# A channel-attention and highway kernel: score banks, load groups, chain order and the last store rearranged

## The chip, the cores and the metric

The kernel runs on one core of a Trainium2 chip. The metric is the device time of one execution in microseconds; a kernel's time is the median of several runs. The core has five engines, each with an instruction queue of its own that is worked in order: TensorE (PE in the profile; PEld is its weight load), VectorE (DVE), ScalarE (ACT), GpSimd (POOL) and SyncE (SP). DMA engines move data between memory and the core's SBUF; SyncE, ScalarE and GpSimd issue them. TensorE writes into PSUM, of which the kernel uses all eight banks.

## The reference

For each of B = 4 batches of N = 6336 rows and C = 256 columns, the columns of q and k are normalised over the rows, and a 256 by 256 attention over the columns is made and applied to v; a highway layer follows on all 25344 rows:

```
qn = q / (norm(q, axis=1) + 1e-6);  kn = k / (norm(k, axis=1) + 1e-6)
s  = kn^T @ qn / tau;  a = softmax(s)          # (B, 256, 256)
x  = v @ a                                     # (B, N, 256) -> (B*N, 256)
H  = relu(x @ w_h);  T = sigmoid(x @ w_t + b_t)
out = T * H + (1 - T) * x
```

## The kernel before

**Scores.** The 6336 rows of a batch are 49 tiles of 128 rows and one of 64. For each tile j, `emit_score` (L192) adds k^T q to the bank S (two 128 by 256 matmuls), k^T k to the bank G (two 128 by 128), and q^T q to G (two more), whose diagonals are the squared norms. Instead of the two q^T q matmuls, runs of four tiles may be squared on ScalarE (`square`, L395), added on GpSimd and reduced on VectorE; `decide` (L368) chooses as the program is written out. Batches 1 to 3 use the same two banks S and G as batch 0, one after the other.

**Chain.** After a batch's last score, `make_chain` (L436) builds its attention: the norms out of G (VectorE, L448), a copy of S (`ssb`, ScalarE, L463), roots, inverses, a small matmul that spreads the inverse norms of q (`cq`, L502), the scaled logits (L507), exp on ScalarE (L518, with a table load before it and `back`, L603, which loads the sigmoid's table after it), the normalised attention (`softmax`, L524, into `mr`), its transpose (`at`, L539, copied by `at_copy`, L550), and the product of attention and the highway's weights (`ah`, L558, copied by `ahat_copy` into `mr`). With that, a tile of v needs three products alone: v a, v a w_h and v a w_t.

**Slots.** A slot t is a pair of v tiles. Its work: four transposes (T, L234) into one PSUM bank, a copy to SBUF (C, L248), twelve 256-column matmuls into Z, H and X (the gate's, the hidden and the plain product, `mains`, L253), the sigmoid on ScalarE (tt, L301), a refill of the Z bank with the bias (seed, L304), two operations on VectorE (th, L309 and ux, L317), a subtraction on GpSimd (L335; the last one on VectorE) and a store for each four pairs (L351, from SyncE's queue; the last four pairs each have their own). There are 25 slots a batch; in batch 3 the slot with the 64-row tile comes 21st. Z has two banks of its own; H and X take the oldest free bank of a list, hx0 to hx2 (`free_bank`, L278), which `cq`, `at` and `ah` share. After the last chain, S and G join this list (L1014).

**Order.** The instruction order is written out by a planner at build time (L995 on): it steps through time with lengths that the program gives each task, and each engine takes the first task of its lists that is ready. TensorE (`step_pe`, L903) prefers chain tasks, then scores that are due, then transposes, then the slot's matmuls. A score of batch b + 1 is due at a slot that `slot_of_score` (L631) spreads evenly up to `S_END`, so that a batch's scores run between the slots of the batch before it. On the chip, each engine follows its list in order and waits where the data are late.

**Loads.** q, k and v are loaded by GpSimd in groups of tiles (`QG`, `VG`, L95), with a conversion from f32 to f16; q and k have four buffers each, v three. A load waits until the scores (or transposes) have read the group four (three) before. The list `order` (L624) fixes the order of the loads: after batch 0's groups the first group of batch 1, then the two weights, the first group of v, the next group of batch 1, and so on. A store can be put behind a GpSimd instruction, so as to leave the DMA engines to the loads.

Of the kernel before, what the change touches and what calls it, by code (L numbers as in the profile page):

```python
# [60 lines left out]
def kernel(  # L61
# [33 lines left out]
    QG = [spans(4, 8, 8, 8, 8, 8, 3, 2)] + [spans(4, 12, 12, 12, 9)] * (B - 1)  # L95
# [11 lines left out]
    S_END = [19, 44, 69]  # L107
# [84 lines left out]
    def emit_score(b, j):  # L192
        if j == 0:
            S_t[b] = psum_pool.tile([P, 2, C], f32, tag="S", name=f"S{b}")
            G_t[b] = psum_pool.tile([P, 4, P], f32, tag="G", name=f"G{b}")
# [78 lines left out]
    banks = [Bank(f"hx{n}") for n in range(3)]  # L274
    late_banks = [Bank("S"), Bank("G")]
    in_late = [False]

    def free_bank(now):  # L278
        pool = banks + (late_banks if in_late[0] else [])
        got = [x for x in pool if x.free(now)]  # L280
        if not got:
            return None
        return min(got, key=lambda x: max([t.end for t in x.until], default=-1.0))
# [57 lines left out]
    def emit_store(b, i0, n, behind):  # L341
# [6 lines left out]
        else:  # L348
            parts = [(rows(ob)[:, 2 * i0 : 2 * (i0 + n), :], ot[:, o0 : o0 + 2 * n, :])]
        for dst, src in parts:  # L350
            dma = nc.sync.dma_start(out=dst, in_=src)  # L351
# [84 lines left out]
    def make_chain(b):  # L436
# [166 lines left out]
        add("back", "ACT", 1.5, lambda e: preload_table(Act.Sigmoid), [(T["exps", 1], 0.0)])  # L603
        for c in range(2):
            add(("softmax", c), "DVE", 0.5, softmax(c), [(T["exps", c], LAG)])
            add(("at", c), "PE", 2 * MM(P), pe_at(c), [(T["softmax", c], TO_PE)],
                bank=lambda c=c: [T["atc", c]])
            add(("atc", c), "DVE" if c == 0 else "ACT", 0.4, at_copy(c), [(T["at", c], PE_LAG)])
            add(("ah", c), "PE", 2 * MM(2 * C), pe_ahat(c), [(T["atc", c], TO_PE)],
                bank=lambda c=c: [T["ahc", c]])  # L610
            add(("ahc", c), "ACT" if c == 0 else "DVE", 0.62, ahat_copy(c),
                [(T["ah", c], PE_LAG)])
        return T
# [14 lines left out]
    order += [(-80, "q", 1, 0), (-80, "k", 1, 0), (-79, "w", 0, 0), (-79, "w", 0, 1)]  # L628
    order += [(-70, "v", 0, 0), (-69, "remv", 0, 0), (2, "remq", 0, 1), (2, "remk", 0, 1)]

    def slot_of_score(b, j):  # L631
        lo = (b - 1) * NPAIR - 1 if b > 1 else -3
        return lo + (S_END[b - 1] - lo) * j / NS

    for b in range(1, B):
        for g in range(len(QG[b])):
            if (b, g) == (1, 0):
                continue
# [126 lines left out]
    for b in range(B):  # L765
        for j in range(NS + 1):
            t = score[b, j]
            if j == 0 and b > 0:
                t.after += [(chains[b - 1]["norms"], TO_PE), (chains[b - 1]["ssb"], TO_PE)]

    for t in range(NSLOT):
# [27 lines left out]
        queues["PE.out"] += [Z[t], H[t], X[t]]  # L799
# [103 lines left out]
    def step_pe(now):  # L903
# [10 lines left out]
        if look < 2 and take("PE.T", "PE", now):  # L914
# [10 lines left out]
    def step_act(now):  # L925
# [4 lines left out]
        if ptr["copy"] - slot_now() < ahead and take("copy", "ACT", now, 0.58):  # L930
# [136 lines left out]
```

## Time and profile before

| | us |
|---|---|
| median of 3 runs (277.8 to 278.63) | 278.09 |
| the profiled execution | 278.24 |
| its span, first to last instruction | 276.5 |
| TensorE busy, 2656 matmuls | 252.2 (91%) |
| weight loads busy | 219.0 (79%) |
| VectorE busy | 203.7 (74%) |
| GpSimd busy | 198.0 (72%) |
| ScalarE busy | 173.1 (63%) |
| 23 stores of 1024 KB, median from issue to landing | 9.7 |
| mean granted clock of TensorE (1 is full) | 0.990 |

The profiled execution took 278.24 us, 1.7 more than its span. All times in the text are counted from the span's start, in this one execution. Busy is the time in which at least one instruction of the engine is drawn; the ends of matmuls are modelled, and neighbours overlap. A row of the timeline gives the start, the length, the engine, the line and operation, what is written and read, and in brackets the idle time before it and what ended it. A row by stage gives the stretch, its length, the busy time of PE, PEld, DVE, ACT and POOL with their instructions, the granted clock, the DMA engines' share and what they moved in GB/s. In the slices, each digit is the busy share of one of 40 equal slices in tenths.

### The profile page before, as it was taken

To read this page: it belongs to the slowest core of one execution; us is meant where nothing else is said; L and a number is where in the kernel's file an instruction comes from. 1 tells how busy PE (TensorE), PEld (TensorE's weight loads), DVE (VectorE), ACT (ScalarE), POOL (GpSimd) and SP (SyncE) were. 2 spreads that over 40 slices of the span, in tenths; PEclk is the share of its full clock that TensorE was granted. 3 is DMA by queue.
4 is the path that set the end of the run, shared out by engine and by line. 5 is a ranking of instruction groups with operands and counts; after the bars stand their busy time and mean duration, and the time that the engine had idled before them with its cause. 6 is when DMAs were issued, how large, how long until landed. Compare 5 with 4: busy or idle time off the path is not lost.

```text
span 276.5 us, 6636 instructions
## 1 busy us (share of the span) xinstructions
PE 252.2 (91%) x2656; PEld 219.0 (79%) x2656; DVE 203.7 (74%) x422; ACT 173.1 (63%) x286; POOL 198.0 (72%) x208
## 2 busy tenths in 40 slices
PE   0997887999999999999999999999999979999980
PEld 0696774889899886999999985999999857999770
DVE  2000046598969789979888887989988899998891
ACT  3300036676666487957656587667775787999850
POOL 5133552789979656998998575998898368888870
PEclk9999999999999999999999999999999999999996
DMA  7999999999999999999999999999999997594353
GB/s 213 216 211 216 202 212 213 214 213 215 214 217 215 247 268 275 269 296 297 265 244 219 287 247 256 281 294 288 284 213 259 373 313 243 88 310 191 152 218 117
DMA packets 15281, 66.10 MB, mean 239 GB/s; under 512 B 1681, under 2 KB 4242, under 8 KB 12306
## 3 DMA queue, kind: packets, MB, share of 16 engines
q0 software_dynamic: 10176, 38.67, 70.5%
q1 hardware_dynamic: 4930, 26.48, 24.1%
q10 hardware_dynamic: 144, 0.52, 0.5%
q8 instruction: 21, 0.34, 0.4%
q14 instruction: 10, 0.08, 0.1%
HBM read 78.38 MB, written 25.95 MB: 377 GB/s over the span
## 4 chain that ended last, share of the span: by engine, by line
PE 68%; DMA 20%; DVE 6%; ACT 1%; issue 1%; POOL 1%; DVEq 0%
PE x L258 13%; PE zbank L258 13%; PE h L258 13%; DMA k<-in_k_dram 13%; PE S L203 12%; PE vtps L234 6%; PE G L206 6%; DMA v<-in_v_dram 6%; PE G L212 3%; DMA qk<-in_k_dram 2%; DVE th L309 1%; DVE vts L248 1%; DVE mr L532 1%; DVE ux L317 1%; DVE ssb L507 1%
## 5 line engine op out<-in xcount | busy, mean ns | idle before, releaser
L335 POOL TENSOR_TENSOR o<-th,ux 128x512 f32<-128x512 f32 x95 | 121.7, 1296 | 33.1 <-DVE ux L317 31.2
L258 PEld LDWEIGHTS <-vts 128*128 128x128 f16 x1200 | 111.7, 98 | 17.9 <-issue 5.8
L301 ACT ACTIVATE tt<-zbank 128x512 f32<-128x512 f32 x100 | 59.4, 597 | 52.8 <-PE zbank L258 30.8
L203 PE MATMUL S<-q,k 128*128 128x256 f16 x392 | 82.1, 279 | 11.0 <-ACT k L753 6.4
L309 DVE SCALAR_TENSOR_TENSOR th<-h,tt 128x512 f32<-128x512 f32 (+1 forms) x104 | 68.8, 665 | 18.2 <-ACT tt L301 14.1
L206 PE MATMUL G<-k 128*128 128x128 f16 x392 | 74.1, 223 | 0.6 <-DVE junk L448 0.6
L317 DVE SCALAR_TENSOR_TENSOR ux<-tt,x 128x512 f32<-128x512 f32 (+1 forms) x104 | 67.9, 656 | 1.8 <-PE x L258 1.8
L258 PE MATMUL zbank<-mr,vts 128*128 128x256 f16 (+1 forms) x400 | 60.7, 273 | 0.7 <-DVE mr L573 0.7
L258 PE MATMUL x<-mr,vts 128*128 128x256 f16 (+1 forms) x400 | 60.5, 273 | 0.4 <-DVE ssb L507 0.4
L258 PE MATMUL h<-mr,vts 128*128 128x256 f16 (+1 forms) x400 | 60.5, 273 | 0.0
L304 ACT COPY zbank<-btb 128x512 f32<-128x512 f32 x98 | 57.8, 590 | 2.9
L203 PEld LDWEIGHTS <-k 128*128 128x128 f16 x392 | 39.1, 100 | 16.7 <-ACT k L753 6.4
L206 PEld LDWEIGHTS <-k 128*128 128x128 f16 x392 | 39.2, 100 | 1.8 <-issue 0.8
L234 PE MATMUL vtps<-ident,v 128*128 128x128 f16 x392 | 38.2, 219 | 1.7 <-DVE vts L248 1.4
L248 DVE COPY vts<-vtps 128x512 f16<-128x512 f16 x85 | 35.5, 418 | 5.2 <-PE vtps L234 4.3
L403 POOL TENSOR_TENSOR sq<-sq 128x512 f32<-128x512 f32 (+1 forms) x25 | 30.1, 1208 | 4.3 <-ACT sq L397 4.2
L234 PEld LDWEIGHTS <-v 128*128 128x128 f16 x392 | 27.7, 98 | 5.3 <-issue 3.4
L448 DVE SCALAR_TENSOR_TENSOR junk<-G,ident 128x128 f32<-128x128 f32 x16 | 4.7, 291 | 32.8 <-PE G L212 32.3
L212 PE MATMUL G<-q 128*128 128x128 f16 x192 | 27.4, 226 | 0.0
L154 POOL DMA_DIRECT2D q<-in_q_dram x22 | 12.2, 552 | 20.0 <-PE G L212 18.9
L397 ACT ACTIVATE sq<-q 128x1024 f32<-128x1024 f16 x25 | 26.2, 1054 | 0.0
L410 DVE TENSOR_REDUCE sq<-sq 128x256 f32<-128x768 f32 x25 | 25.7, 1029 | 0.5 <-POOL sq L403 0.3
(67 smaller groups left out, 138.7 us busy)
## 6 DMA issues: line engine op xcount, KB each, us to landing
out_dram<-o SPq DMA_DIRECT2D x23, 1024.0 KB, 9.7
v<-in_v_dram POOLq DMA_DIRECT2D x10, 768.0 KB, 15.8
q<-in_q_dram POOLq DMA_DIRECT2D x9, 768.0 KB, 21.4
k<-in_k_dram POOLq DMA_DIRECT2D x9, 768.0 KB, 22.5
v<-in_v_dram POOLq DMA_DIRECT2D x4, 832.0 KB, 20.6
q<-in_q_dram POOLq DMA_DIRECT2D x5, 512.0 KB, 11.1
k<-in_k_dram POOLq DMA_DIRECT2D x5, 512.0 KB, 13.1
q<-in_q_dram POOLq DMA_DIRECT2D x3, 576.0 KB, 23.7
```

Of the source, the lines that this page charges most:

```text
L203: nc.tensor.matmul(S[:, c, :], kc, qq[0:nr, :], start=first and c == 0, stop=last and c == 1)
L206: nc.tensor.matmul(G[:, c, :], kc, kc, start=first and c == 0, stop=False, skip_group_check=True,)
L212: nc.tensor.matmul(G[:, 2 + c, :], qc, qc, start=False, stop=last and c == 1, skip_group_check=True)
L234: nc.tensor.transpose(ps[:, u, c, 0:r], vt[0:r, bass.ts(c, P)], ident[0:r, 0:r])
L248: cp(out=sb, in_=ps)
L258: nc.tensor.matmul(dst[0:r, u, :], vT_t[t][:, u, kt, 0:r], mr[:, kt, off : off + C], start=(not seeded and kt == 0 and (u == 0 or i == NPA ...
L301: nc.scalar.activation(out=tts[t], in_=zbank[t % 2], func=Act.Sigmoid)
L304: nc.scalar.copy(out=zbank[t % 2], in_=btb)
L309: nc.vector.scalar_tensor_tensor(out=ths[t][pr, us, :], in0=hx["h", t][pr, us, :], scalar=0.0, in1=tts[t][pr, us, :], op0=AluOp.max, op1=A ...
L317: nc.vector.scalar_tensor_tensor(out=uxs[t][pr, us, :], in0=tts[t][pr, us, :], scalar=1.0, in1=hx["x", t][pr, us, :], op0=AluOp.subtract, ...
L335: ins = sub.tensor_tensor(out=ot[pr, o0 + us.start : o0 + us.stop, :], in0=ths[t][pr, us, :], in1=uxs[t][pr, us, :], op=AluOp.subtract,)
L403: nc.gpsimd.tensor_tensor(out=sq[:, 1 : 1 + half, :], in0=sq[:, 1 : 1 + half, :], in1=sq[:, 1 + CH - half : 1 + CH, :], op=AluOp.add,)
```

## The change

- Batch 1's scores get the banks hx1 and hx2 instead of S and G, and batches 2 and 3 use those too. The list of banks for H, X and the chain's products begins with hx0 alone; S and G join it when batch 0's chain has read them, hx1 and hx2 when the last chain has.
- Batch 1's scores no longer wait for batch 0's norms and copy of S. Batch 1's groups of q and k are 4, 4, 12, 12, 12 and 5 tiles instead of 4, 12, 12, 12 and 9, and the second group is loaded ahead of the weights and the first v.
- Scores are due one slot earlier (`S_END` 18, 43, 68 for 19, 44, 69), and the spread of a batch's scores begins after the end of the batch before it.
- In the chain, both softmax steps stand ahead of the copies of `at`, and both `at` ahead of both `ah`; in batch 0, the sigmoid's table is loaded after the copies of `ah`.
- During slot 0, ScalarE and VectorE hold back v copies and square runs where a chain task is soon due.
- The last store is issued from ScalarE's queue. The last slot's Z matmuls stand ahead of the X matmuls of the slot before, and in the last six slots transposes may run three slots ahead.

```diff
--- before.py
+++ after.py
@@ -92,7 +92,8 @@
         assert s0 == NS
         return got
 
-    QG = [spans(4, 8, 8, 8, 8, 8, 3, 2)] + [spans(4, 12, 12, 12, 9)] * (B - 1)
+    QG = [spans(4, 8, 8, 8, 8, 8, 3, 2), spans(4, 4, 12, 12, 12, 5)]
+    QG += [spans(4, 12, 12, 12, 9)] * (B - 2)
     VG = [spans(8, 8, 8, 12, 13)] + [spans(12, 12, 12, 13)] * (B - 1)
     GT = {"q": 12, "k": 12, "v": 13}
     CH = 4
@@ -104,7 +105,7 @@
     OG = 4
     LASTS = list(range(20)) + [NPAIR - 1] + list(range(20, NPAIR - 1))
     PAIRS = [list(range(NPAIR))] * (B - 1) + [LASTS]
-    S_END = [19, 44, 69]
+    S_END = [18, 43, 68]
 
     ctx.enter_context(tc.manual_schedule())
     const_pool = ctx.enter_context(tc.tile_pool(name="consts", bufs=1))
@@ -191,8 +192,9 @@
 
     def emit_score(b, j):
         if j == 0:
-            S_t[b] = psum_pool.tile([P, 2, C], f32, tag="S", name=f"S{b}")
-            G_t[b] = psum_pool.tile([P, 4, P], f32, tag="G", name=f"G{b}")
+            tags = ("S", "G") if b == 0 else ("hx1", "hx2")
+            S_t[b] = psum_pool.tile([P, 2, C], f32, tag=tags[0], name=f"S{b}")
+            G_t[b] = psum_pool.tile([P, 4, P], f32, tag=tags[1], name=f"G{b}")
         nr = REM if j == NS else P
         kk, qq = tile_of("k", b, j), tile_of("q", b, j)
         S, G = S_t[b], G_t[b]
@@ -271,13 +273,11 @@
         def free(self, now):
             return all(t.end is not None and t.end + LAG <= now for t in self.until)
 
-    banks = [Bank(f"hx{n}") for n in range(3)]
-    late_banks = [Bank("S"), Bank("G")]
-    in_late = [False]
+    banks = [Bank("hx0")]
+    handed = []
 
     def free_bank(now):
-        pool = banks + (late_banks if in_late[0] else [])
-        got = [x for x in pool if x.free(now)]
+        got = [x for x in banks if x.free(now)]
         if not got:
             return None
         return min(got, key=lambda x: max([t.end for t in x.until], default=-1.0))
@@ -347,8 +347,9 @@
             ]
         else:
             parts = [(rows(ob)[:, 2 * i0 : 2 * (i0 + n), :], ot[:, o0 : o0 + 2 * n, :])]
+        queue = nc.scalar if (b, i0 + n) == (B - 1, NPAIR - 1) else nc.sync
         for dst, src in parts:
-            dma = nc.sync.dma_start(out=dst, in_=src)
+            dma = queue.dma_start(out=dst, in_=src)
             if behind is not None:
                 tc.add_manual_dep(
                     dma.ins, behind.ins.name,
@@ -600,16 +601,24 @@
             add(("logits", c), "DVE", 0.38, logits(c), [(T["cq"], PE_LAG), (T["ssb"], LAG)])
             add(("exps", c), "ACT", 0.72 + (1.3 if c == 0 and b > 0 else 0), exps(c),
                 [(T["logits", c], LAG), (T["invs", "k"], LAG)])
-        add("back", "ACT", 1.5, lambda e: preload_table(Act.Sigmoid), [(T["exps", 1], 0.0)])
+        back = lambda: add("back", "ACT", 1.5, lambda e: preload_table(Act.Sigmoid),
+                           [(T["exps", 1], 0.0)])
+        if b > 0:
+            back()
         for c in range(2):
             add(("softmax", c), "DVE", 0.5, softmax(c), [(T["exps", c], LAG)])
+        for c in range(2):
             add(("at", c), "PE", 2 * MM(P), pe_at(c), [(T["softmax", c], TO_PE)],
                 bank=lambda c=c: [T["atc", c]])
+        for c in range(2):
             add(("atc", c), "DVE" if c == 0 else "ACT", 0.4, at_copy(c), [(T["at", c], PE_LAG)])
             add(("ah", c), "PE", 2 * MM(2 * C), pe_ahat(c), [(T["atc", c], TO_PE)],
                 bank=lambda c=c: [T["ahc", c]])
+        for c in range(2):
             add(("ahc", c), "ACT" if c == 0 else "DVE", 0.62, ahat_copy(c),
                 [(T["ah", c], PE_LAG)])
+        if b == 0:
+            back()
         return T
 
 
@@ -625,16 +634,17 @@
     for g in range(len(QG[0])):
         order += [(-100 + g, "q", 0, g), (-100 + g, "k", 0, g)]
     order += [(-94.5, "remq", 0, 0), (-94.5, "remk", 0, 0)]
-    order += [(-80, "q", 1, 0), (-80, "k", 1, 0), (-79, "w", 0, 0), (-79, "w", 0, 1)]
+    order += [(-80, "q", 1, 0), (-80, "k", 1, 0), (-79, "q", 1, 1), (-79, "k", 1, 1)]
+    order += [(-78, "w", 0, 0), (-78, "w", 0, 1)]
     order += [(-70, "v", 0, 0), (-69, "remv", 0, 0), (2, "remq", 0, 1), (2, "remk", 0, 1)]
 
     def slot_of_score(b, j):
-        lo = (b - 1) * NPAIR - 1 if b > 1 else -3
+        lo = S_END[b - 2] + 1 if b > 1 else -3
         return lo + (S_END[b - 1] - lo) * j / NS
 
     for b in range(1, B):
         for g in range(len(QG[b])):
-            if (b, g) == (1, 0):
+            if b == 1 and g < 2:
                 continue
             at = slot_of_score(b, QG[b][g][0]) - 1.0
             order += [(at, "q", b, g), (at, "k", b, g)]
@@ -765,7 +775,7 @@
     for b in range(B):
         for j in range(NS + 1):
             t = score[b, j]
-            if j == 0 and b > 0:
+            if j == 0 and b > 1:
                 t.after += [(chains[b - 1]["norms"], TO_PE), (chains[b - 1]["ssb"], TO_PE)]
 
     for t in range(NSLOT):
@@ -796,7 +806,9 @@
             if n >= ORING:
                 for s in store_of_group[o_groups[n - ORING]]:
                     SUB[t].after.append((s.dma, LAG))
-        queues["PE.out"] += [Z[t], H[t], X[t]]
+        queues["PE.out"] += [Z[t], H[t], X[t]] if t < NSLOT - 1 else [H[t], X[t]]
+        if t == NSLOT - 1:
+            queues["PE.out"].insert(len(queues["PE.out"]) - 3, Z[t])
         queues["PE.T"].append(TR[t])
         queues["copy"].append(CP[t])
         queues["ACT.tt"].append(TT[t])
@@ -911,7 +923,7 @@
             if b == 0 or slot_of_score(b, j) <= t:
                 if take("PE.S", "PE", now):
                     return True
-        if look < 2 and take("PE.T", "PE", now):
+        if look < (2 if t < NSLOT - 6 else 3) and take("PE.T", "PE", now):
             return True
         if take("PE.out", "PE", now):
             return True
@@ -927,13 +939,16 @@
             if take(n, "ACT", now):
                 return True
         ahead = 3 if slot_now() >= ACT_COPIES and ptr["copy"] % 2 == 0 else 1
-        if ptr["copy"] - slot_now() < ahead and take("copy", "ACT", now, 0.58):
+        wait = slot_now() == 0 and soon("ACT", now, 0.58)
+        if not wait and ptr["copy"] - slot_now() < ahead and take("copy", "ACT", now, 0.58):
             return True
-        return not soon("ACT", now, 1.05) and take("ACT.sq", "ACT", now)
+        return slot_now() > 0 and not soon("ACT", now, 1.05) and take("ACT.sq", "ACT", now)
 
     def step_dve(now):
         if take("DVE.chain", "DVE", now):
             return True
+        if slot_now() == 0 and soon("DVE", now, 0.42):
+            return False
         ahead = 1 if slot_now() >= ACT_COPIES and ptr["copy"] % 2 == 0 else 3
         if ptr["copy"] - slot_now() < ahead and take("copy", "DVE", now, 0.42):
             return True
@@ -941,7 +956,7 @@
             return True
         if take("copy", "DVE", now, 0.42):
             return True
-        return not soon("DVE", now, 1.0) and take("DVE.red", "DVE", now)
+        return slot_now() > 0 and not soon("DVE", now, 1.0) and take("DVE.red", "DVE", now)
 
     landing = []
     nload = [0]
@@ -1011,11 +1026,12 @@
             seed_banks()
             preload_table(Act.Sqrt)
             setup_done[0] = True
-        if not in_late[0] and chains[B - 1]["norms"].end is not None and \
-                chains[B - 1]["ssb"].end is not None:
-            in_late[0] = True
-            late_banks[0].until = [chains[B - 1]["ssb"]]
-            late_banks[1].until = [chains[B - 1]["norms"]]
+        for b, key, tag in ((0, "ssb", "S"), (0, "norms", "G"), (B - 1, "ssb", "hx1"),
+                            (B - 1, "norms", "hx2")):
+            if tag not in handed and chains[b][key].end is not None:
+                handed.append(tag)
+                banks.append(Bank(tag))
+                banks[-1].until = [chains[b][key]]
         for e, f in (("PE", step_pe), ("ACT", step_act), ("DVE", step_dve),
                      ("POOL", step_pool), ("SP", step_sp)):
             while free[e] <= now and f(now):
```

## The prediction

> **What bounds the kernel now.** I read the page's shares and slices first, then busy time by stage, then TensorE's timeline where a stage lost time, then the chain that ended last and the landing times of the loads.
>
> ```profile
> PE 252.2 (91%) x2656; PEld 219.0 (79%) x2656; DVE 203.7 (74%) x422; ACT 173.1 (63%) x286; POOL 198.0 (72%) x208
> ...
> PE   0997887999999999999999999999999979999980
> ...
> DMA  7999999999999999999999999999999997594353
> ```
>
> Two resources are full at once: TensorE from about 37 us to the end, the DMA engines up to slice 33 (228 us). By stage (sum of PE busy is the first figure after the length; the last two are DMA share and GB/s):
>
> ```profile
> 37.40:51.50 14.10, 10.61 (x101) 7.72 (x99) 8.58 (x30) 10.23 (x19) 5.30 (x8) 1.00 1.10 212
> ...
> 95.80:111.00 15.20, 14.59 (x145) 11.38 (x143) 13.90 (x37) 11.60 (x21) 8.81 (x10) 1.00 1.04 271
> ...
> 156.00:173.00 17.00, 16.31 (x163) 12.82 (x161) 14.55 (x39) 13.52 (x25) 10.04 (x12) 1.00 1.04 257
> 173.00:215.00 42.00, 42.00 (x467) 38.57 (x465) 38.34 (x65) 28.87 (x44) 36.73 (x33) 1.00 1.02 267
> 215.00:231.00 16.00, 14.33 (x127) 10.42 (x125) 15.06 (x45) 12.57 (x23) 9.61 (x9) 1.00 0.94 318
> ```
>
> After 37.4 us TensorE idles only where a batch's softmax chain runs: 3.49 us in batch 0's, 0.61, 0.69 and 1.67 in the others. A 256-column matmul is drawn 0.27 long but issued every 0.11, so each wait costs about 0.16 more than its drawn idle: 8, 3, 3 and 5 waits make 4.8, 1.1, 1.1 and 2.5 us lost. The first chain, in TensorE's timeline:
>
> ```profile
> 37.27 0.27 PE L212 MATMUL G<-rem_q 64*128 64x128 f16 x2
> 38.05 0.27 PE L203 MATMUL S<-q,k 128*128 128x256 f16 x1 [0.51 <-ACT ssb L463]
> 38.94 0.22 PE L206 MATMUL G<-k 128*128 128x128 f16 x1 [0.62 <-DVE junk L448]
> ...
> 40.15 0.65 PE L502 MATMUL cq<-dcat,taus 128*128 128x256 f32 x2
> ...
> 41.22 0.40 PE L234 MATMUL vtps<-ident,v 128*128 128x128 f16 x4
> 42.13 0.38 PE L234 MATMUL vtps<-ident,v 128*128 128x128 f16 x4 [0.52 <-DVE vts L248]
> ...
> 46.47 0.49 PE L258 MATMUL zbank<-mr,vts 128*128 128x256 f16 x3 [0.67 <-DVE mr L573]
> ```
>
> Batch 1's first scores wait for batch 0's to leave the two banks: (0.51 + 0.16) + (0.62 + 0.16) = 1.45 us. But loads pace TensorE here too, as the chain in order of time (start, length) shows, and late q/k loads have little to spare; the load of batch 3's last k group, issued at 179.1, is the 26.1 below and lands at 205.2, and its first score starts at 206.1:
>
> ```profile
> 36.17 15.58 DMA v<-in_v_dram
> 52.04 22.01 DMA k<-in_k_dram
> ```
>
> ```profile
> L154 POOL DMA_DIRECT2D k<-in_k_dram x1: 550/550/550, 179.1 to 179.1; - x1
> ...
> DMA to landing us min/median/max: 23.6/24.8/26.1
> ```
>
> [...]what stands behind a waiting one waits too, and the trace agrees (G at 38.94 holds all scores after it). [...]no trace before shows a store on ScalarE's queue.[...] the trace's four-matmul groups start 0.44 apart[...].
>
> **Early stage, 37.4 to 76.5.** Removed: the 1.45 us. Added: a 4-tile q and k group (q1_1, k1_1) ahead of the weights and v. In the trace 38 tiles' worth of bytes (64 KB each) landed between 37.12 and 49.07, 0.314 us a tile. So k1_1 lands at 37.12 + 8 x 0.314 = 39.6, the weights at 40.9, the first v at 43.4 (41.2 before), k1_2 at 51.6. The changed program's order is scores 0-5, cq, scores 6-7, at0, T0, at1, ah0, ah1, T1, gates. Scores 0-3 take 37.4 to 39.1 (0.43 each); 4-5 wait 0.6 for k1_1 and end at 40.4; cq is behind them, so 0.25 later than the 40.15 before. From cq to the first at of before is 42.72 - 40.15 = 2.57 us: at0 at 43.0, after cq and two scores (1.1 us), an idle of 1.4. T0 waits 0.3 for v, ah0 and ah1 0.3, the first gate 0.7 for the copy of ah1, the third slot 0.5 for a bank that th and ux free. Sum 3.8 to 4.0 where 4.8 was: -0.9. The loads cap it: scores 32 on need k1_4, by which 8 more tiles have landed than at the k load of 74.05 before, 74.05 + 8 x 0.31 = 76.5. The old program does the same work (one more slot 1.31, one transpose 0.22, four more unsquared scores 1.75) by 74.1 + 3.3 = 77.4. Gain 0.8. Bounds: loss 0.5, if k1_1's queue has a bubble of 1.3 us; gain 2.0, if T0 and the third slot wait for nothing.
>
> **Chains.** Both softmaxes now precede the at copy on VectorE, and both at precede both ah on TensorE. In batch 1's order, cq is followed on TensorE by 5.05 us of other work until at0, while softmax 0 ends about 4.7 after cq (logits from 0.64, 1.28 table load, two exps), and at1 has 1.5 us more between. I find no wait left but the slow issue at the 64-row tile, which stays. I take 1.0 of 1.1 for batch 1 and 0.8 of 1.1 for batch 2, where one score group comes close to its load. Bounds: nothing, and 2.2. ACT's sq.2.4 (1.05) now stands ahead of batch 1's exps, covered by those 5.05. For batch 3, T74 waits for a copy behind softmax 1, 1.15 us, and T75 for another, 0.57: 1.7 where 2.5 was, -0.8; bounds 0 and -2.0.
>
> **Squares.** The order shows one more run (26 of them for 25): 8 G matmuls of 0.055 go from TensorE, -0.44. It adds 1.05 to ACT, 1.2 to POOL and 1.03 to VectorE, which are 63, 72 and 74% busy; without that cover at most +1.0.
>
> **Tail.** The last four stores land in 3.6 to 4.2 us each, 0.6 apart as they are issued, so they queue behind nothing; the last is issued at 270.64, right after the last subtract. From ScalarE's queue, empty by then, the same: 0 (0.6 at most if rings do queue; -0.2 to lose). The last Z ahead of the previous X lets tt start 0.44 sooner, but VectorE is back to back from 266.75 with th, ux, th, ux and the subtract; th waits 0.06 for tt now. -0.1. X98 slips 0.44, to end when ux98 can take it.
>
> **Loads in the second half.** Scores end one slot earlier, so they need q and k sooner. The order of k3_4 and v2_3 (13 tiles) is exchanged, so k3_4 lands 13 x 0.31 = 4.0 earlier, 201.2. From there the old program needs 276.5 - 206.1 = 70.4; the new one has five gate groups (2.19) and a transpose (0.22) more to do after it, and 0.9 less of waits: the span cannot end before 201.2 + 71.9 = 273.1. The terms so far, -0.8 - 1.8 - 0.8 - 0.44 - 0.1 = -3.94, give 272.6. With this and k3_1 and k3_3, moved alike, I add 0.8 (bounds 0 and 4).
>
> Sum: -3.14 on a profiled run of 278.24 (span 276.5, 1.7 around it) gives 275.1; the median of the runs is 278.09, 0.15 lower, so 275.0.
>
> **Rivals.** (a) The chains and the early stage give all that they lose, loads keep up: 2.0 + 2.2 + 1.2 + 0.4 = 5.8, about 272.3. For: covers are long. Against: DMA share above 1.0 until 210. 0.20. (b) k1_1 arrives a microsecond late and cq with it, so the chain of batch 0 slips whole: the early gain turns into a loss of 0.5, 276.3. For: it is issued at 35.1 behind a ring slot and the queue is short then. 0.15. (c) Loads take back everything: TensorE only moves its idle time to batches 2 and 3, 278, within 0.3%. 0.10. (d) Slower: stores, which start as TensorE runs ahead, take the place that k3_4 gained. Break-even is a first score of k3_4 at 276.5 - 71.9 = 204.6; from 205.4 on it is slower by over 0.3% (0.83 us, about what a measurement can tell). At 206.5 it gives 280. Against: stores keep their places behind the subtracts. 0.10.
>
> **How the numbers follow.** The forecast has 0.45. Faster: 0.45 + 0.20 + 0.15 = 0.80; same 0.10; slower 0.10. The range leaves out (d) and the best of (a): 272.5 to 278.3.
>
> **What would show it.** Scores without a gap at 37.4, then a short wait for k at 39.1; T0 after 43.4; batch 1's and 2's chains with under 0.3 us idle; PE matmuls 2648; k3_4 landing near 201 with its score right behind it; the last store 3.6 us from issue to landing. Wrong if k1_1 lands after 41, or if TensorE waits over 1 us for k in batches 2 and 3.

## The result and the profile after

The changed kernel takes 278.32 us (median of 4 runs, 278.19 to 278.45) where the kernel before takes 278.01 beside it (4 runs, 277.8 to 278.63). The ratio is 1.0007, 95% interval 0.999 to 1.0025: no difference, where 275.0 was forecast. The profiled execution after took 278.45 us with a span of 276.7; before, 278.24 and 276.5. Runs of one kernel fall into groups some 1 to 2 us apart, so a median also depends on how many runs fell into each, and I give spans where it matters.

From the page of the kernel after, the shares and the slices that answer to those of before:

```profile
PE 252.1 (91%) x2648; PEld 218.8 (79%) x2648; DVE 205.9 (74%) x422; ACT 174.4 (63%) x288; POOL 200.5 (72%) x211
...
PE   0997886999999989999999999999999979999980
...
DMA  7999999999999999999999999999999989783352
```

The eight matmuls are gone and every other total is within 3 us of what it was. By stage (columns as in the prediction: stretch, its length, PE, PEld, DVE, ACT, POOL busy, granted clock, DMA share, GB/s; the first row is a stretch that the prediction did not show):

```profile
30.00:40.00 10.00, 8.33 (x108) 7.54 (x108) 2.19 (x14) 1.84 (x4) 5.95 (x11) 1.00 1.07 179
37.40:51.50 14.10, 10.72 (x95) 7.77 (x93) 7.37 (x27) 8.22 (x17) 6.31 (x12) 0.88 1.12 207
95.80:111.00 15.20, 13.81 (x148) 11.71 (x146) 14.32 (x36) 10.08 (x18) 9.68 (x11) 1.00 1.04 275
156.00:173.00 17.00, 16.56 (x178) 13.86 (x176) 16.20 (x41) 12.79 (x22) 11.05 (x12) 1.00 1.03 270
173.00:215.00 42.00, 41.98 (x454) 37.79 (x453) 37.79 (x69) 29.38 (x46) 35.89 (x32) 1.00 1.02 270
215.00:231.00 16.00, 14.46 (x129) 10.97 (x128) 14.72 (x41) 13.13 (x24) 9.80 (x10) 1.00 0.94 294
```

Batch 0's chain idles 3.38 us (3.49 before), batch 1's 1.39 (0.61 before), batch 2's 0.44 (0.69), batch 3's 1.54 (1.67). A gain in two chains has paid for a loss in another, and the idle time of the early stage has stayed where it was. Two readings matter: the 179 GB/s of the first row, and in the second row the clock of 0.88, where before had 1.00. The first row in the kernel before:

```profile
30.00:40.00 10.00, 7.79 (x100) 7.05 (x101) 2.17 (x14) 1.85 (x4) 7.15 (x12) 1.00 1.19 206
```

To count in one currency, I take each matmul at its undisturbed issue time (the median from start to start: 109 ns for 256 columns and 56 for 128 in both traces, 216 for 512 in that of after) and call TensorE's time beyond that a loss. The two f32 matmuls of a cq I counted at 0.43 us each, twice what the traces show (they issue them 0.22 apart), so every row with a chain stands 0.4 us too low, before and after alike. A stretch without a wait can come out below nothing (-0.31 in a row of before), so I take each figure as good to about 0.3 us. Losses in us:

| stretch | before | after | predicted change | change |
|---|---|---|---|---|
| 37.4 to 80, early stage | 5.78 | 6.25 | -0.8 | +0.5 |
| 80 to 120, chain of batch 1 | 1.39 | 2.10 | -1.0 | +0.7 |
| 120 to 173, chain of batch 2 | 1.54 | 0.63 | -0.8 | -0.9 |
| 173 to 215 | -0.31 | 0.35 | +0.8 for loads | +0.7 |
| 215 to 240, chain of batch 3 | 3.29 | 2.83 | -0.8 | -0.5 |
| matmuls saved | | | -0.44 | -0.45 |

The sum is +0.05, and the span's end, below, adds 0.16: 0.2, which is the difference of the two spans. These are two executions; in others with the same loads (runs 1, 5, 9 and 12) the early stage loses 5.8 to 6.5 us, so there it is nothing to 0.7 us worse than before, and nowhere better.

**Where the early stage went.** TensorE's timeline of the kernel after:

```profile
40.43 0.28 PE L205 MATMUL S<-q,k 128*128 128x256 f16 x1 [0.99 <-DMA k<-in_k_dram]
...
41.10 0.65 PE L503 MATMUL cq<-dcat,taus 128*128 128x256 f32 x2
...
43.55 0.28 PE L544 MATMUL at<-ident,mr 128*128 128x128 f16 x2 [1.14 <-DVE mr L533]
...
44.93 0.40 PE L236 MATMUL vtps<-ident,v 128*128 128x128 f16 x4 [1.10 <-DMA v<-in_v_dram]
```

The scores run without a gap from 37.4 on, as meant. Then they wait 0.99 for k1_1, which lands at 40.4 and not at 39.6; cq follows at 41.10 (40.15 before), and T0 waits 1.10 for a v that lands at 44.9 (43.4 forecast, 41.2 before). The loads are late because of their queue. GpSimd's issues in the kernel after, and then in the kernel before:

```profile
35.11 0.53 POOL L155 DMA_DIRECT2D q<-in_q_dram  x1 [3.24 <-PE G L214]
...
36.15 0.75 POOL L751 DMA_DIRECT2D wht<-in_moe_w_h_dram  x1
...
37.58 0.58 POOL L155 DMA_DIRECT2D v<-in_v_dram  x1
```

```profile
31.84 0.73 POOL L741 DMA_DIRECT2D wht<-in_moe_w_h_dram  x1
...
33.28 0.56 POOL L154 DMA_DIRECT2D v<-in_v_dram  x1
```

The load of q1_1 (batch 1's second group of q) waits 3.24 us for batch 0's matmuls to free a q buffer, and the weights and v, which need no q buffer, stand behind it. They go out 4.3 us later than before. In that gap the DMA engines run short, at 179 GB/s for 206: over 10 us that is 270 KB, 4.1 tiles of 64 KB, or 1.3 us at the prediction's 0.314 us a tile, an estimate.

**Where batch 1's chain went.** The chain in order of time (start, length) of the kernel after:

```profile
98.51 1.81 DVE dcat L494 x2
100.47 0.67 PE cq L503 x2
...
158.12 1.34 DVE dcat L494 x2
159.50 0.70 PE cq L503 x2
```

The two scalings that make `dcat` (an identity times the inverse norms, 128 by 128 each) take 1.81 and 1.34 us together. The same instructions before and after, by tile (minimum, median and maximum in ns):

```profile
L493 DVE TENSOR_SCALAR dcat<-ident,inv x8: 279/284/288, 39.2 to 218.2; 128x128 f32<-128x128 f32 x8
```

```profile
L494 DVE TENSOR_SCALAR dcat<-ident,inv x8: 274/286/1130, 39.2 to 217.0; 128x128 f32<-128x128 f32 x8
```

Nothing about them is changed but the moment. GpSimd's timeline after, at that moment:

```profile
98.28 1.28 POOL L335 TENSOR_TENSOR o<-th,ux 128x512 f32<-128x512 f32 x1
99.52 0.72 POOL L404 TENSOR_TENSOR sq<-sq 128x256 f32<-128x256 f32 x1
```

The first dcat starts at 98.51, 0.23 after a subtract; the subtract ends at 99.56, and 0.08 later, at 99.64, so does dcat (1.13 us). The second ends at 100.32, behind the addition that ended at 100.24. At 158.12 the same happens with one subtract. Before, none of the eight dcat had GpSimd arithmetic beside it. So it is VectorE that waits: each of these three dcat ends 0.08 to 0.09 us behind the GpSimd operation that was under way, while the subtracts beside them take 1.28 us, as they do elsewhere (1.29 on the average of 95). What in the hardware makes it wait the trace doesn't show. So cq waited 1.19 and 0.60 us, by start to start, with all of TensorE's later work behind it. `mr`, the same kind of instruction, meets a subtract in both kernels: at 104.72 it takes 1.38 us after, where 0.35 is its time alone, and at 104.54 0.91 us before.

### The profile page after: what moved, and what is told of

Read it like the earlier page. It is cut to its first block, busy times and chain, and to the rows that moved or that the text cites. A ratio compares the mean times of both kernels' runs of the same rounds, so it can differ in the third digit from the quotient of the medians.

```text
span 276.7 us, 6628 instructions
## 1 busy us (share of the span) xinstructions
PE 252.1 (91%) x2648; PEld 218.8 (79%) x2648; DVE 205.9 (74%) x422; ACT 174.4 (63%) x288; POOL 200.5 (72%) x211
## 4 chain that ended last, share of the span: by engine, by line
PE 73%; DVE 11%; DMA 9%; ACT 2%; issue 2%; POOL 1%; DVEq 0%
PE x L260 14%; PE zbank L260 13%; PE h L260 13%; PE S L205 13%; PE vtps L236 7%; PE G L208 6%; DMA k<-in_k_dram 5%; DMA v<-in_v_dram 3%; DVE th L309 2%; PE G L214 2%; DVE ux L317 2%; DVE vts L250 2%; DMA qk<-in_k_dram 2%; PE ah L563 2%; DVE dcat L494 1%
## 5 line engine op out<-in xcount | busy, mean ns | idle before, releaser
L404 POOL TENSOR_TENSOR sq<-sq 128x512 f32<-128x512 f32 (+1 forms) x26 | 31.4, 1209 | 1.7 <-ACT sq L398 1.6
L155 POOL DMA_DIRECT2D q<-in_q_dram x23 | 12.9, 561 | 25.2 <-PE G L214 21.7
L411 DVE TENSOR_REDUCE sq<-sq 128x256 f32<-128x768 f32 x26 | 26.7, 1028 | 0.9 <-POOL sq L404 0.9
L398 ACT ACTIVATE sq<-q 128x1024 f32<-128x1024 f16 x26 | 27.1, 1054 | 0.0
L214 PE MATMUL G<-q 128*128 128x128 f16 x184 | 26.3, 226 | 0.0
```

Of the source, the lines that this page charges most:

```text
L214: nc.tensor.matmul(G[:, 2 + c, :], qc, qc, start=False, stop=last and c == 1, skip_group_check=True)
L404: nc.gpsimd.tensor_tensor(out=sq[:, 1 : 1 + half, :], in0=sq[:, 1 : 1 + half, :], in1=sq[:, 1 + CH - half : 1 + CH, :], op=AluOp.add,)
```

## The experiments

**1. dcat of batches 1 and 2 on ScalarE.** In the kernel after:

```diff
                     for c in range(2):
+                        if b in (1, 2):
+                            nc.scalar.mul(dcat[:, c, :], ident0, st["inv"][:, 2 + c : 3 + c])
+                            continue
                         nc.vector.tensor_scalar(
```

> The changed kernel, in which the two dcat products of batches 1 and 2 are made by ScalarE instead of VectorE. Theory P (VectorE's dcat at 98.5 and 158.1 was 1.13 us long instead of 0.28 because GpSimd ran an elementwise operation beside it, and cq and all TensorE work behind cq waited for it, 1.19 and 0.60 us): dcat takes about 0.3 each, TensorE's waits before cq in batches 1 and 2 go, and the time falls by 1.3 to 1.8, to 276.5 to 277.0. Rival Q (the order of the chain on VectorE makes cq late whatever dcat costs, or loads take the time back later): cq still waits 0.5 or more, or TensorE waits for k or v instead, and the time stays within 0.3 of 278.3.

Measured: 277.34 us (20 runs), ratio to before 0.9964 (0.9947 to 0.998), span 275.4. ScalarE took 0.39 us for each dcat, no wait stands ahead of cq in batches 1 and 2, and batch 1's stretch idles 0.45 instead of 1.39 us. The collision of dcat cost about 1 us. This run doesn't tell yet whether the form of VectorE's instruction or something else about VectorE was slow.

**2. TensorE kept busy in batch 0's chain** (20 more transposes ahead of slot 0's, 10 more matmuls ahead of `at`, all without effect on the output):

```diff
+        for _ in range(20 if t == 0 else 0):
+            nc.tensor.transpose(ps[:, 0, 0, :], ident, ident)
...
+                for _ in range(10 if (b, ic) == (0, 0) else 0):
+                    nc.tensor.matmul(at[:, 1, :], ident, zeros[:, 0:C], start=True, stop=True)
```

> The changed kernel, in which TensorE does 10 unused matmuls ahead of the first at and 20 unused transposes ahead of T0, in the two gaps of 1.30 and 1.26 us of batch 0's chain (extra work that leaves the result as it is). Theory C (the granted clock of 0.5 from 45.7 to 49.1 us followed on the low activity of these gaps, and it costs the time): the clock stays at 1.0 there, and the time falls by 0.9, to 277.4. Rival L (loads pace this stage): the clock stays at 1.0, slot 0 starts 0.5 to 0.9 earlier, but the scores behind k1_3 and k1_4, which had 0.4 and 0.5 us to spare, then wait for k, and the time falls by 0.5 at most, to 277.8 to 278.3. If the clock still falls to 0.5, activity in the gaps is not its cause.

Measured: 278.31 us (12 runs), ratio 1.0003 (0.9983 to 1.0023). The clock stayed at 1.00 from 45.7 to 49.1, and what that gave was lost to waits for k at 53.25 and 66.5 us. So the lower clock of the second row above explains none of the result: the loads set the pace until about 80 us. Runs 1, 9 and 12, with the same loads and the clock at 1.00 there, agree: they lose 5.8 to 6.5 us up to 80 us where after has 6.25. That the added matmuls kept the clock up this run alone can't show, since those three have none (more on this in the last section).

**3. Weights and the first v ahead of q1_1 and k1_1.** In the kernel after:

```diff
-    order += [(-80, "q", 1, 0), (-80, "k", 1, 0), (-79, "q", 1, 1), (-79, "k", 1, 1)]
+    order += [(-80, "q", 1, 0), (-80, "k", 1, 0)]
     order += [(-78, "w", 0, 0), (-78, "w", 0, 1)]
     order += [(-70, "v", 0, 0), (-69, "remv", 0, 0), (2, "remq", 0, 1), (2, "remk", 0, 1)]
+    order += [(-68, "q", 1, 1), (-68, "k", 1, 1)]
```

> The changed kernel with the weights and the first v loaded ahead of batch 1's second q and k group again (that part alone undone; the plan from batch 1's chain on is the same). Theory B (the second group waits for a free buffer until 35.1 us, and with everything else behind it the DMA engines run dry for about 1 us near 37; the first v is 3.7 us later for it, and the first chain waits for v): first v at about 41.2, the moved bytes between 30 and 40 us back from 179 to 206 GB/s, k1_4 at 76.4 instead of 77.4, slot 0 a microsecond or more earlier; the time falls by 0.4 to 0.9, to 277.4 to 277.9. Rival L0 (the early stage is worth nothing either way because the end is set by the later chains): TensorE waits elsewhere, 278.3 within 0.2.

Measured: 277.42 us (20 runs), ratio 0.9957 (0.9942 to 0.9972). The DMA engines are full again in the stretch that had run short:

```profile
30.00:40.00 10.00, 8.55 (x109) 7.79 (x110) 2.17 (x14) 1.90 (x4) 6.99 (x12) 1.00 1.19 206
```

T0 starts at 41.06 instead of 44.93, and the loss from 37.4 to 80 us is 3.90 us where after has 6.25. Only 0.9 us of these 2.35 show in the median, 1.9 in the shortest span (274.5 for 276.4): in the profiled run the clock was halved from 222.0 to 225.4, in batch 3's chain, which cost about 1.4 us there (a loss of 4.25 from 215 to 240, after 2.83).

**4. The banks alone** (before with batches 1 to 3 in hx1 and hx2 and the list of banks as in the change; loads, chain and end as before):

```diff
-            S_t[b] = psum_pool.tile([P, 2, C], f32, tag="S", name=f"S{b}")
-            G_t[b] = psum_pool.tile([P, 4, P], f32, tag="G", name=f"G{b}")
+            tags = ("S", "G") if b == 0 else ("hx1", "hx2")
+            S_t[b] = psum_pool.tile([P, 2, C], f32, tag=tags[0], name=f"S{b}")
+            G_t[b] = psum_pool.tile([P, 4, P], f32, tag=tags[1], name=f"G{b}")
```

> The kernel before with one part of the change: batch 1's scores (and those of batches 2 and 3) in banks of their own, without the wait for batch 0's norms and copy of S; groups, load order, due slots and chain order as before. Theory G (the gap of 1.45 us at 38 us is on the path): 276.6. Theory L (loads pace TensorE up to the k load of 74.05, which had nothing to spare): the gap at 38 us is gone, TensorE waits for k at 49.1, 60 and 74 us by as much more, and the time falls by 0.8 at most, to 277.2 to 278.0.

Measured: 279.44 us (20 runs), ratio 1.0012 (0.999 to 1.0034). The gap at 38 us is gone and nothing is won; in the profiled run the clock was halved for 6.8 us from 43.5. The shortest span is 275.7 us, that of before beside it 275.9. In the profiled run TensorE waits 0.66 us for the first v at 40.95, a wait that before didn't have; the waits for k at 49, 60 and 74 us that theory L named aren't in this trace, and that the loads take back the rest is argued from run 2, not shown.

**5. The two scalings in another form**, in the kernel after; every engine's instructions stay in the same order:

```diff
-                        nc.vector.tensor_scalar(
-                            out=dcat[:, c, :], in0=ident0, scalar1=st["inv"][:, 2 + c : 3 + c],
-                            scalar2=None, op0=AluOp.mult, op1=AluOp.bypass,
+                        nc.vector.scalar_tensor_tensor(
+                            out=dcat[:, c, :], in0=ident0, scalar=st["inv"][:, 2 + c : 3 + c],
+                            in1=ident0, op0=AluOp.mult, op1=AluOp.mult,
```

and `mr` likewise with `in1=st["ssb"][:, c, :]` and a bypass.

> The changed kernel with the same instructions in the same order on every engine; only the form of VectorE's 8 dcat and 8 mr scalings is another: SCALAR_TENSOR_TENSOR with a second SBUF operand in place of TENSOR_SCALAR. Theory P (the fast form of TENSOR_SCALAR waits for a GpSimd operation that is under way, other forms don't): dcat and mr take 0.28 to 0.45 us also beside GpSimd, the waits of 1.19 and 0.60 us before cq of batches 1 and 2 go, 277.1 us (276.8 to 277.5). Rival W (what is slow is VectorE's traffic to SBUF beside GpSimd, whatever the form): dcat stays at 0.8 to 1.1 us in batches 1 and 2, 278.3 us.

Measured: 280.19 us (18 runs), ratio 1.0063 (1.0045 to 1.0082). By tile:

```profile
L494 DVE SCALAR_TENSOR_TENSOR dcat<-ident,inv x8: 339/352/1212, 39.1 to 217.6; 128x128 f32<-128x128 f32 x8
```

The wait is still there (up to 1.21 us for one dcat), and each scaling is 0.07 to 0.13 us slower besides. Theory P as I put it, "other forms don't", falls: this form, with two inputs in SBUF where TENSOR_SCALAR has one, waits as well. The profiled span is 0.9 us over that of after, lost in the chains of batches 1, 2 and 3 (0.37, 0.27 and 0.36), where mr takes 0.48 for 0.35 as well; the rest of the 1.9 us between the medians I have not traced (the shortest spans are 277.0 and 276.4).

**6. Runs 3 and 5 together.**

> The changed kernel with weights and the first v ahead of the second q and k group of batch 1, and with the other form of the dcat and mr scalings. If the two losses are separate places of the same path, the gains add: 277.4 of the first alone less 1.2, 276.2 us (275.8 to 276.7). If the time won early is lost again before the chain of batch 1 (loads pace the scores), or the first gain already hid the waits before cq: 277.2 us.

Measured: 279.27 us (22 runs), ratio 1.0028 (1.0009 to 1.0048). With the form that waits, the waits before cq are 1.31 and 0.75 us, so the second gain doesn't come. That of the loads does: up to 80 us the loss is 4.95 where run 5 has 5.99, and the shortest span is 275.2 where run 5 has 277.0, 1.8 less (1.9 in run 3). In the profiled run the clock was halved in two chains, at 43.2 and 224.2.

**7. The chain's steps in the old order**, all else as in the change:

```diff
-        back = lambda: add("back", "ACT", 1.5, lambda e: preload_table(Act.Sigmoid),
-                           [(T["exps", 1], 0.0)])
-        if b > 0:
-            back()
+        add("back", "ACT", 1.5, lambda e: preload_table(Act.Sigmoid), [(T["exps", 1], 0.0)])
         for c in range(2):
             add(("softmax", c), "DVE", 0.5, softmax(c), [(T["exps", c], LAG)])
-        for c in range(2):
             add(("at", c), "PE", 2 * MM(P), pe_at(c), [(T["softmax", c], TO_PE)],
...
```

> The changed kernel with the chain's steps back in the old order (softmax 0, at 0, softmax 1, at 1, each copy behind its own; the table's return early in batch 0 too). Theory C (the new order is worth what the losses at the chains of batch 2 and 3 fell by, 0.6 and 0.45 us, and the collision with GpSimd in batch 1 is a matter of where its operations fall, so the old order may miss it): 278.3 to 279.4 us, 279.0 if the collisions stay. Rival N (the order of the chain's steps is worth nothing; the collision is all that it made): the waits before cq are under 0.3 us and the time is 277.2 us.

Measured: 279.01 us (22 runs), ratio 1.002 (1.0005 to 1.0036); against the 1.0007 of the change the intervals overlap. The profiled run lost 8.0 us from 37.4 to 80, with the clock halved for 6.8 us and T0 waiting 2.3 us for v, so its total says little on the order. From 80 to 173 it loses 3.1 us. One dcat still falls beside a GpSimd operation (1.15 us, and cq 0.62 late in batch 1), and `at` and the transposes of v wait as in the kernel before (0.63 us at 166.5). The change loses 2.7 there with 1.79 us of waits for dcat, and run 1, with the new order and none of them, 1.3. Without its 0.62 the old order has 2.5, so in these two batches the new one is worth some 1.2 us. In batch 3's chain the traces with the old order (before, runs 4, 7 and 8) lose 3.2 to 3.5 us, those with the new one, the forms of the change and full clock there (after, runs 1 and 13) 2.6 to 2.9. Theory C is nearer.

**8. The end alone**, in the kernel before: last store from ScalarE's queue, last Z ahead, look-ahead of the last transposes.

```diff
+        queue = nc.scalar if (b, i0 + n) == (B - 1, NPAIR - 1) else nc.sync
...
-            dma = nc.sync.dma_start(out=dst, in_=src)
+            dma = queue.dma_start(out=dst, in_=src)
```

> The kernel before with the edits of the end alone: last store issued from ScalarE's queue, last Z ahead of its slot, and look-ahead of transposes in the last six slots. Theory T (the last store's own landing time sets the end, not who issues it): 278.0 us (277.8 to 278.2), the last store lands 3.5 to 4.2 us after its issue as before. Rival (the issue slot counted): 0.3 us less, 277.7 us.

Measured: 278.53 us (22 runs), ratio 1.0015 (1.0 to 1.003), span 276.5 as before: no gain, as expected. But the store landed 2.1 us after its issue at 270.67, not 3.5 to 4.2, and the span didn't end sooner. Theory T had the right number for a wrong reason; runs 12 and 13 follow from it. (In the same trace the store before it, which SyncE issues at 270.12, lands in 2.0 us, and in run 4, where SyncE issues the last store, that one lands in 2.1 us as well, so the issuer isn't what made it faster.)

**9. A form with an accumulator output**, in the kernel after. As before it reads one operand from SBUF; a read of the accumulator follows each (0.08 us):

```diff
-                            scalar2=None, op0=AluOp.mult, op1=AluOp.bypass,
+                            scalar2=0.0, op0=AluOp.mult, op1=AluOp.add, accum_out=unused,
```

for dcat, and the same for mr.

> The changed kernel with the 8 dcat and 8 mr scalings as TENSOR_SCALAR with an accumulator output: one operand read from SBUF, and an accumulator read more (0.08 us each in the other rows that have one). Theory P2 (VectorE waits for a running GpSimd operation[...]; a form with one SBUF input doesn't): dcat and mr stay under 0.45 us beside GpSimd, waits before cq of batches 1 and 2 under 0.6 and 0.3 us, 277.2 us (276.8 to 277.7). Rival W (any VectorE operation from SBUF to SBUF waits, and only the move to ScalarE helped): dcat at 1.1 us again, 278.5 us.

Measured: 277.5 us (22 runs), ratio 0.9978 (0.9957 to 0.9998). By tile:

```profile
L494 DVE TENSOR_SCALAR_CACHE_REDUCE dcat<-ident,inv x8: 345/346/347, 39.3 to 215.7; 128x128 f32<-128x128 f32 x8
```

GpSimd's subtract and the two dcat of batch 1, from the timelines of the two engines:

```profile
97.97 1.30 POOL L335 TENSOR_TENSOR o<-th,ux 128x512 f32<-128x512 f32 x1
98.21 0.35 DVE L494 TENSOR_SCALAR_CACHE_REDUCE dcat<-ident,inv 128x128 f32<-128x128 f32 x1
98.60 0.35 DVE L494 TENSOR_SCALAR_CACHE_REDUCE dcat<-ident,inv 128x128 f32<-128x128 f32 x1
```

Same engine, same moment, same size, and no wait: 0.35 us each, where TENSOR_SCALAR took up to 1.13 (after) and the form with two inputs in SBUF up to 1.21 (run 5). With run 1, where ScalarE took 0.39, this shows that the wait belongs to the form of VectorE's instruction while GpSimd works; what is behind it in the hardware none of the three runs shows. TensorE now idles nowhere in the stretches of batches 1 and 2 (15.20 of 15.20 and 17.00 of 17.00 us busy): mr, which meets a subtract at 103.35, takes 0.48 us as all eight do (478 to 480 ns), and the wait of `at` for it (106.2 in the change, 105.1 in run 1) is gone too. Part of the gain comes back as a wait of 1.03 us for a k load at 202.5.

**10 and 11. Loads as in run 3, with dcat and mr as in run 9 or dcat as in run 1.**

> Weights and the first v ahead of the second q and k group, and the form with an accumulator output for dcat and mr. P2 with gains that add: 277.4 less 1.0, 276.4 us (275.9 to 276.9). If the early gain is lost again before the chains, or the form waits as well: 277.4 us.

> Weights and the first v ahead of the second q and k group, and dcat of batches 1 and 2 on ScalarE. If the losses are two separate places of one path the gains add (277.4 less 1.0 to 1.2): 276.3 us (275.8 to 276.8), no wait before cq in batches 1 and 2. If the lower clock in the chain of batch 3 takes it back: 277.4 us.

Measured: 275.83 us (7 runs), ratio 0.9916 (0.9882 to 0.9949), for run 10, and 275.35 us (7 runs), ratio 0.99 (0.9864 to 0.9936), for run 11. The two losses are separate places of one path, and the gains add: the shortest spans are 276.4 us after, 275.0 in run 1, 274.5 in run 3 and 273.2 in run 11, so 1.4 and 1.9 make 3.3, and 3.2 is measured. Neither kernel has a wait before cq in batches 1 and 2.

**12. One more subtract off GpSimd**, in the kernel after:

```diff
-    DVE_SUBS, ACT_COPIES = 1, 77
+    DVE_SUBS, ACT_COPIES = 2, 77
```

The trace of the end, first of before and then of after: the operations on the program's last line (minimum, median and maximum in ns, then first and last start).

```profile
L1062 POOLq DRAIN  x3: 45/102/7017, 268.7 to 276.2; - x3
```

```profile
L1078 POOLq DRAIN  x3: 45/102/7153, 268.7 to 276.4; - x3
```

GpSimd's queue comes to a drain (an instruction at the program's end) at 268.7, which lasts 7.02 us before, until 275.7, and 7.15 after, until 275.9. In its last microseconds nothing else happens, as the stretch of the kernel after shows:

```profile
273.00:275.00 2.00, 0.00 (x0) 0.00 (x0) 0.00 (x0) 0.00 (x0) 0.00 (x0) 0.50 0.00 0
```

The last store has landed at 272.8.

> The changed kernel with the subtract of the last slot but one on VectorE as well (two there, one fewer on GpSimd). In the traces so far GpSimd's end-of-program drain ends 5.69 us (kernels with the loads of before) or 5.85 us (with those of after) after its last subtract, and 0.75 us after the drain the span ends. Theory E (this drain sets the end, not the last store): GpSimd's last subtract ends 1.25 us earlier, the last store lands 0.7 us later, the span is 1.2 us shorter, 277.1 us. Rival S (the last store sets the end, as the prediction took it): 0.7 us longer, 279.0 us.

Measured: 277.55 us (22 runs), ratio 0.9974 (0.9958 to 0.999). In the profiled run TensorE's last matmul came 1.2 us later than in after (the clock was halved once in batch 3's chain) and the span ended at 276.6 all the same, 6.6 us after GpSimd's last subtract, as in after. Twelve of its runs have spans of 275.0 to 275.7; the four of after have 276.4 to 276.7. Theory E holds, S doesn't.

**13. All three: run 11 with run 12's edit.**

> Weights and the first v ahead of the second q and k group, dcat of batches 1 and 2 on ScalarE, and one more of the last subtracts on VectorE. Theory E: the profiled span is 1.2 us shorter than without the last edit at the same clock, 274.2 us (273.8 to 275.5, the upper end if the clock falls once more). Rival S: 276.0 us.

Measured: 273.97 us (6 runs), ratio 0.9845 (0.9813 to 0.9877), span 272.3: about 1.5% faster than the kernel before. The instruction behind its drain starts 5.85 us after the last subtract on GpSimd, as in after. The chains of batches 1 and 2:

```profile
95.80:111.00 15.20, 14.75 (x151) 11.70 (x149) 13.36 (x29) 12.24 (x22) 9.75 (x12) 1.00 1.04 266
156.00:173.00 17.00, 17.00 (x176) 13.89 (x174) 15.79 (x35) 14.24 (x25) 11.97 (x13) 1.00 1.04 260
```

## Why the prediction was wrong

**Early stage: the arrival of the loads failed.** The step "38 tiles' worth of bytes (64 KB each) landed between 37.12 and 49.07, 0.314 us a tile. So k1_1 lands at 37.12 + 8 x 0.314 = 39.6" took the old rate for a queue that had a hole. The prediction knew that q1_1 is issued at 35.1 behind a buffer (rival b) but counted only that load as late; what it moved the load past, the weights and v, waited with it. k1_1 came at 40.4, the weights at 42.4, v at 44.9, k1_2 at 53.0, k1_4 at 77.4: 0.8 to 1.5 us later than forecast. The gain of 0.8 became a loss of 0.5 in this execution, and of nothing to 0.7 in others. With these loads in a better order (run 3) the stage gains 1.9 on before. The cap by the loads was seen rightly (run 2), and the banks alone bring nothing (run 4). Rival (b) was the right one for this stage: k1_1 0.8 late, cq 0.95 later than before, and a loss. The two waits at 38 us did go with the other banks; they came from batch 1's scores going into S and G while the chain still read them (0.51 us for the copy of S and 0.62 for the norms in the trace of before; in run 4, with other banks alone, the scores run from 37.27 to 38.93 without a gap).

**Chain of batch 1: the step "I find no wait left" failed.** The waits that it meant to remove did go: the 0.34 to 0.39 us each before `x`, a v transpose and `at` (of these, 0.52 us at 106.2 for mr came back, beside a subtract). In their place came 1.19 us before cq, since dcat fell beside GpSimd's work; the predicted -1.0 became +0.7. It asked what is queued behind cq and not what GpSimd does beside VectorE's step. The trace of before had a hint: mr, a TENSOR_SCALAR too, took 0.35 us alone and up to 0.91 beside a subtract. Run 9 shows what it hangs on: in another form dcat takes 0.35 us beside the same subtract. The rest of the step was sound: with the new order and no wait for dcat (run 1), batches 1 and 2 lose 1.3 us where before lost 2.9, 1.6 less for the 1.8 forecast.

**Chain of batch 2: right in sum** (-0.8 forecast, -0.9), in part by luck: cq waited 0.60 there as well, and more had been removed than the prediction counted. (Its idle time of before, 0.69 and three times 0.16, makes 1.2, not the 1.1 that it started from.) **Chain of batch 3: direction right, size off**: -0.5 for -0.8, since T74 still waits 0.95 and T75 0.33, and ah 0.49. Run 7, with the old order, loses 3.2 there where before loses 3.3, which fits that the order gave it; the difference is little more than the figures are good to.

**Squares: right**, 2648 matmuls and 0.45 us.

**Tail: a number near nothing, as measured, for a wrong reason.** It took the last store's landing for the end. GpSimd's drain ends later, and a store that lands 1.5 us sooner (272.8 for 274.25) moved nothing. The drain also ends 0.16 us later behind its last subtract with the changed loads (5.85 for 5.69), which the forecast of -0.1 didn't have.

**Loads in the second half: right number by luck.** k3_4 landed at 202.2 (201.2 forecast) and no score waited for a load after 80 us, so the term of +0.8 had nothing to stand on. The loss of 173 to 215 did rise, by 0.7, in small gaps of which none exceeds 0.26 us; their cause stays open. In runs 1 and 9, where TensorE comes earlier, a wait for a k load at 202.5 to 202.7 does appear (0.39 and 1.03 us).

The forecast was 3.3 us short: by the table some 1.3 in the early stage, 1.7 in batch 1's chain and 0.3 in batch 3's.

## What to carry to other kernels

Before a load is moved up in a queue, look at when its buffer comes free: everything behind it leaves no earlier (here the load waited 3.24 us, and the weights and v went out 4.3 us later), and the DMA engines can run short although their mean rate is high (179 GB/s for 206 here). When a chain's steps are reordered, lay VectorE's operations of the forms that waited here (TENSOR_SCALAR, 1.13 us for 0.28, and SCALAR_TENSOR_TENSOR with two inputs in SBUF, 1.21 for 0.35) over GpSimd's timeline; if they can meet, ScalarE (0.39 us for 0.28) or the form with an accumulator (0.35, and 0.08 to read it) costs 0.1 to 0.2 us and saved about 1 here. And look at the last microseconds of the trace for what is still running when nothing moves: the end may belong to an engine that is thought to be idle, as here to GpSimd, whose drain takes 7.02 us before and 7.15 after.

## What the runs showed that I had not expected

- After GpSimd's drain at the end of the program, the next instruction of its queue starts 5.69 us after its last subtract in the kernels with the loads of before (before, runs 4 and 8) and 5.85 us in those with the loads of after, to within 0.01 us in all fifteen traces. The latter have two more loads on GpSimd's queue; whether these make the 0.16 us wasn't tried.
- The granted clock of TensorE falls to 0.50 for 3.41 us (or twice that: 6.8 in run 4, from 43.5 to 50.3), most often in a chain, in some executions. Where it falls differs from one to the next; rows of the kernel after, of run 3 and of run 2, as above:

```profile
45.70:49.10 3.40, 3.25 (x15) 1.84 (x15) 1.11 (x3) 2.77 (x5) 0.81 (x2) 0.50 1.02 210
```

```profile
222.00:225.40 3.40, 3.40 (x14) 1.94 (x13) 2.50 (x5) 2.17 (x4) 2.80 (x3) 0.50 0.77 125
```

```profile
224.60:228.00 3.40, 3.40 (x17) 2.10 (x15) 2.91 (x6) 1.71 (x3) 2.47 (x2) 0.50 0.94 155
```

What sets it off wasn't shown; how empty a chain leaves TensorE doesn't decide it alone. By the matmuls' undisturbed issue times, an estimate, the 3.41 us ahead of the halved clock hold 0.26 of their length in matmuls in after (from 42.3) and 0.34 in run 3 (from 218.6). But in batch 3's chain a stretch of that length holds 0.31 before (from 222.3) and 0.33 after (from 220.8), and the clock stays at 1.00 in the 3.4 us behind either.

What it costs depends on the place. In batch 0's chain it is nothing that shows with the loads of after (run 2). With those of run 3 it is 0.8 to 1.0 us: the traces in which it fell there (runs 6, 10, 11 and 13) lose 4.7 to 4.9 us up to 80 us, run 3 itself, at full clock, 3.9. In batch 3's chain the five traces in which it fell there (runs 2, 3, 6, 11 and 12) lose 4.3 to 4.8 us from 215 to 240, the ten others 2.6 to 3.5.
